# Values' steps before the keys', PSUM banks shared three and three, products one slot later

## The chip, the cores and the metric

The kernel runs on one NeuronCore of a Trainium2 chip. The metric is the device time of one execution in microseconds (us). Engines are named as in the profile: PE is the matrix engine's matmuls and PEld its weight loads, DVE, ACT and POOL are the vector, scalar and GpSimd engines, SP issues most DMAs.

## The reference

Three stages follow one another, all in fp32.

1. Attention: q, k, v are (8 batches, 8 heads, 576 positions, 64). Keys and values are averaged over groups of 8 positions, so that 72 pooled rows stand in each batch and head. `attn = softmax(q @ k_p.T / 8)`, output `attn @ v_p`. With the heads side by side it gives x, 4608 tokens by 512.
2. A dense layer: `h = x @ w_in` (512 to 2048), `g = max(0.01 * h, h)`, `y = g @ w_out` (2048 to 512).
3. A mixture of eight experts: `argmax(y @ w_gate)` picks one expert per token, which computes `max(y @ w1[e], 0) @ w2[e]` (512 to 1024 to 512), scaled by the softmax weight of the expert that was picked.

## The kernel before

**Precision.** Each fp32 operand of a large matmul is kept as a high part and a low part in a reduced format that PE takes at full rate, and a product is three matmuls (high by high, high by low, low by high). So nearly each result that leaves PSUM is written twice: ACT copies the high part (`act_copy`, L132), DVE subtracts it from the source for the low part (`sub`, L135).

**Slots.** Tokens are cut into 18 blocks of 256 (two tiles of 128). For each block b and each of 16 slices f of the hidden width there is one slot (b, f). The order is written out by hand in `seq`: blocks 0 and 1 are interleaved at the start, while the weights are converted; from b = 2 on the slots run in order. One turn of the main loop (from L1221) issues:

- `g1(b, f)`: 12 matmuls of 256 columns into one PSUM bank h; ACT writes 0.01 h to an SBUF tile g, DVE takes the maximum (L509; for b of 2 and more the result stays in the bank);
- the hooks of this slot (`run_slot`), set by `plan()` with `at(slot, function, ...)`;
- `g2` of an earlier slot (6 matmuls of 512 columns, L529, accumulated over f into the two banks y0 and y1 of the block): the list `pend` holds slots whose product into y is still to come, two of them in general, one at the edge of a block (f = 15 and f = 0);
- at f = 0 `y_evac` of the block before: two ACT copies and a DMA of y;
- `g_hi(b, f)` (ACT) and `g_lo(b, f)` (DVE), which write the two parts of g into one of two `ghl` tiles. `g_lo` is the last reader of the bank h.

All engines take their instructions in program order, so a late DVE instruction holds up everything behind it, and PE waits in turn for the data or the bank that it needs.

**Hooks.** The attention of the tiles of block b runs in the slots of block b-1: with i = 0 or 1 for the tile, `att_a` (4 transposes of q) at f = 0 and 7, `att_b` (scores, L380) at f = 2 and 9, `att_e` (exp) at 3 and 10, `att_n` (normalise, DVE) at 4 and 11, `att_c` (6 transposes, L412 and L418, then two DVE subtractions) at 6 and 13, and `att_av` (the values' product, L439, into x) for both at f = 15. Keys and values of a batch nb are loaded and pooled ahead of its first tile: parts 0 to 3 are keys, parts 4 and 5 the values' first 512 positions, part 6 the values' last 64 (the "rest"). Each part has three steps: `kv_load` (SP: 1, 2 or 8 DMAs), `kv_pool` (three DVE additions, and for part 6 a POOL multiplication, L300, into a further tile), `kv_use` (keys: one PE transpose, L313, and two ACT copies; values: ACT and DVE write `vm`, L325, or in `v_rest` `vr`). Raw parts share two `kv` tiles, so the load of a part waits for the use of the part two before it, and it is issued from that use. `att_b` needs the four keys, `att_av` needs all of `vm` and `vr`. In `plan()`, L1037 to L1056, the four key steps end just ahead of the first tile's `att_b`; the values' three stand 2, 4 and 6 slots after the last key step. For batches 2, 3, 6 and 7, whose first tile is the second of a block, this puts the rest's use into f = 14, one slot ahead of `att_av`. Other hooks: the experts' weights are split all along (`ps_split`: ACT copy, POOL subtraction of 128x512), DVE takes 16 dot products per block for the gate (L549), and small routing steps follow.

**PSUM.** There are eight banks. `pt("att")` hands out a0 and a1 in turn to everything that the hooks do on PE; `pt("h")` hands out h0 and h1, and from slot (2, 6) on y2 and y3 too, which blocks 0 and 1 no longer need. y0 and y1 hold the block's sums. In the profile a bank shows as a, h or y, so a `g1` can write "y".

**Third stage.** From about 1045 us on the experts run on gathered tokens with the same banks and `ghl` tiles: `p_g1`, `p_h`, `p_g2` on pairs of tiles, then single tiles (`m_g1`, `m_hT`, `m_g2`).

Of the kernel before, what the change touches and what calls it, by code (L numbers as in the profile page):

```python
# [21 lines left out]
def kernel(  # L22
# [13 lines left out]
    P = 128  # L36
# [60 lines left out]
    tri = pool.tile([P, P], BF16, name="tri")  # L97
    ones = pool.tile([P, P], BF16, name="ones")
    mask8 = pool.tile([64, E], F32, name="mask8")
    band = pool.tile([P, 112], F32, name="band")  # L100
    rep8 = pool.tile([64, E, E], F32, name="rep8")
    ebase = pool.tile([P, E], F32, name="ebase")
    iota8 = pool.tile([P, E], F32, name="iota8")
    rev8 = pool.tile([P, E], F32, name="rev8")
# [10 lines left out]
    def sb(shape, dt, tag, bufs=1):  # L115
        return (second[0] if tag in ("ps", "kv", "y4") else second[1] if tag in THIRD else pool).tile(shape, dt, name=tag, tag=tag, bufs=bufs)
# [73 lines left out]
    def kv_load(nb, i):  # L190
        if i < 4:
            t = sb([SP, 2, 512], F32, "kv", 2)
            nc.sync.dma_start(
                out=t, in_=k[nb, 2 * i:2 * i + 2].rearrange("h (m r) d -> m h (r d)", r=POOL)
            )
        elif i < 6:
            t = sb([P, 2, 512], F32, "kv", 2)
            for par in range(2):
                h0 = 4 * (i - 4) + par
                nc.sync.dma_start(  # L200
                    out=t[64 * par:64 * par + 64],
                    in_=v[nb, h0:h0 + 3:2, 0:512, :].rearrange("h (m r) d -> m h (r d)", r=POOL),
                )
        else:
            t = sb([64, 1, 512], F32, "kv", 2)
            for h in range(H):
                nc.sync.dma_start(
                    out=t[8 * h:8 * h + 8, 0, :],
                    in_=v[nb, h, 512:576, :].rearrange("(m r) d -> m (r d)", r=POOL),
                )  # L210
        kv_raw[nb, i] = t

    def kv_load0_k(nb):
        kt = sb([SP, H, 512], F32, "w03")
# [75 lines left out]
    def kv_pool(nb, i, eng=None):  # L290
        t = kv_raw[nb, i]
        eng = eng or nc.vector
        for w in (256, 128, 64):
            o = t[:, :, 0:w]
            if w == 64 and i < 4:
                o = t[:, 0, 256:384].rearrange("p (a d) -> p a d", a=2)
            eng.tensor_tensor(out=o, in0=t[:, :, 0:w], in1=t[:, :, w:2 * w], op=ALU.add)  # L297
        if i == 6:
            f = kv_raw[nb, 7] if nb < 2 else sb([64, H, 64], F32, "kv", 2)
            nc.gpsimd.tensor_tensor(  # L300
                out=f,
                in0=t[:, 0:1, 0:64].to_broadcast([64, H, 64]),
                in1=mask8.unsqueeze(2).to_broadcast([64, H, 64]),
                op=ALU.mult,
            )
            kv_raw[nb, 7] = f

    def kv_use(nb, i):
        t = kv_raw.pop((nb, i))
# [180 lines left out]
        act_copy(dh, w)  # L490
        sub(nc.vector, dl, w, f32(dh))

    g_raw, g_hl, y_ps = {}, {}, {}

    def g1(b, f):
        p = pt("h")
        xv = xs(b)
        n = 0
        for kk in range(KD):
            for l, r in ((0, 0), (0, 1), (1, 0)):  # L500
                nc.tensor.matmul(  # L501
                    p[:, 0:BLK], win(f)[:, kk, l], xv[:, kk, r], start=(n == 0), stop=(n == 3 * KD - 1)
                )
                n += 1
        t = sb([P, BLK], F32, "g", 2)
        h = p[:, 0:BLK]
        g = t if b < 2 else h
        act_copy(t, h, 0.01)
        nc.vector.tensor_tensor(out=g, in0=t, in1=h, op=ALU.max)  # L509
        g_raw[b, f] = g  # L510

    def g_hi(b, f):
        hl = sb([P, 2, BLK], F32R, "ghl", 2)
        act_copy(hl[:, 0], g_raw[b, f])
        g_hl[b, f] = hl

# [417 lines left out]
        return b  # L934

    def p_h(p, f, b):
        hl = sb([P, 2, BLK], F32R, "ghl", 2)
        nc.scalar.activation(hl[:, 0], b, AF.Relu)  # L938
        nc.vector.scalar_tensor_tensor(  # L939
            out=hl[:, 1], in0=b, scalar=0.0, in1=f32(hl[:, 0]), op0=ALU.max, op1=ALU.subtract  # L940
        )
        g_hl[p, f] = hl
# [83 lines left out]
    def plan():  # L1026
# [12 lines left out]
        for nb in range(2, B):  # L1039
            t = S * nb // P  # L1040
            b, i = divmod(t, TPB)
            sb_ = (b - 1) * NF + 2 + 7 * i
            use = []
            c = sb_ - 1
            while len(use) < 4:
                if c % NF in (1, 3, 5, 8, 10, 12, 14) and (not use or use[0] - c >= 3):
                    use.insert(0, c)
                c -= 1
            use += [use[3] + 2, use[3] + 4, use[3] + 6]
            for i in range(7):  # L1050
                at(use[i], kv_use, nb, i)
                if i + 2 < 7:
                    at(use[i], kv_load, nb, i + 2)
                at(use[i] - 2 + (i > 3), kv_pool, nb, i)
            at(max(use[0] - 6, 0), kv_load, nb, 0)
            at(use[0] - 5, kv_load, nb, 1)  # L1056
        for i in range(E * NCH):
            s = 34 + i * 9 // 5
            at(s, ps_load, i)
# [62 lines left out]
    with tc.manual_schedule():  # L1122
# [3 lines left out]
        cvp = first.enter_context(tc.tile_pool(name="cvp", bufs=1))  # L1126
        x1 = start.tile([P, KD * 2 * BLK], F32R, name="x1")
        e_t = [start.tile([P, 1024], U32, name=f"e{i}") for i in range(2)]
        ab_t = start.tile([P, 1024], BF16, name="ab_t")
        raw = [cvp.tile([P, 2, 1024], I32, name=f"raw{i}") for i in range(3)]  # L1130
        ebias = sb([P, 1], F32, "ebias")
        nc.vector.memset(ebias, -114688.0 * 65536.0)
# [88 lines left out]
        for s, (b, f) in enumerate(seq):  # L1221
            g1(b, f)
            if late:
                g_lo(*late.pop())
            run_slot(s)
            pend.append((b, f))
            end = s >= 2 * NF - 1 and (s % NF == NF - 1 or s % NF == 0)
            while len(pend) > (1 if end else 2):
                g2(*pend.pop(0))
            if s < 2 * NF:  # L1230
                conv(s, b, f)
            if b > 2 and f == 0:
                y_evac(b - 1)
            if (b, f) == (2, 6):
                banks["h"] += ["y2", "y3"]
            g_hi(b, f)
            if s < 2 * NF + LAG - 1:
                late.append((b, f))
            else:
                g_lo(b, f)  # L1240
            if (b, f) == (1, NF - 1):
                stack.close()
                second.append(ctx.enter_context(tc.tile_pool(name="third", bufs=1, side="right")))
                wgp = ctx.enter_context(tc.tile_pool(name="wgp", bufs=1, side="right"))
                wg_t.append(wgp.tile([P, E, DM], F32, name="wg"))
                nc.sync.dma_start(
                    out=wg_t[0].rearrange("p e d -> p (e d)"),
                    in_=wgT_d.rearrange("e d -> (e d)").partition_broadcast(P),
                )
            k0 = (NB - 1) * NF  # L1250
            if s == k0 + 7:
                early_1()
                w_regs(NR)
            if s == k0 + 12:
                early_2()
            if s >= k0 and f in (9, 10, 11, 15):
                w_load(0, [(9, 10, 11, 15).index(f)], regs[NR][0], None)
# [136 lines left out]
```

## Time and profile before

| | us |
|---|---|
| median of 3 runs | 1524.62 |
| lowest and highest | 1524.16, 1536.25 |
| the profiled execution, whole | 1533.83 |
| its span in the trace | 1532.1 |
| PE, DVE, ACT, POOL busy in it | 1468.8, 929.5, 619.1, 337.5 |

The profiled execution took 1.7 us more than its span. The first 180 us fill the pipeline and convert weights, blocks 2 to 17 of the dense layer take until about 1045 us, the experts the rest. An engine's busy time is the union of its instructions; a wait row says which engine and line sat idle, and whose result ended that. A row of instructions in order of time has start, duration, engine, line, operation, tiles, count, and in brackets the idle time before it.

### The profile page before, as it was taken

The page shows a single profiled execution, that of the slowest core. Times are in us where ns is not written, and L with a number is a line of the kernel's source. Part 1 is how long each engine was busy: PE and PEld are TensorE (multiplying, and loading weights), DVE is VectorE, ACT ScalarE, POOL GpSimd, SP SyncE. Part 2 cuts the span into 40 slices and gives each one's busy share as a digit, 9 for nine tenths or more (in the row PEclk, how much of TensorE's full clock was granted, in tenths as well). Part 3 has the DMA queues.
Part 4 walks back from the last instruction along what each step waited for, and adds up shares of the span by engine and source line. Part 5 has one row for each costly group of instructions (what it writes and reads, how often), then busy time and mean ns, then how long its engine had stood idle before and what let it go on. Part 6 is the DMA issues. An engine that isn't in the chain of part 4 may idle for free. (4 is left out here: it accounts for less than half of the span.)

```text
span 1532.1 us, 25665 instructions
## 1 busy us (share of the span) xinstructions
PE 1468.8 (96%) x9272; PEld 1315.8 (86%) x9272; DVE 929.5 (61%) x2387; ACT 619.1 (40%) x1412; POOL 337.5 (22%) x318
## 2 busy tenths in 40 slices
PE   4698999999999999999999999999999999999998
PEld 3587889999898898899989899988899999988886
DVE  6999588878869888877867867674212112111111
ACT  4666344544444444544444444332222222222222
POOL 4002022222332222222222332111211211201111
PEclk8799999999999999999989999999999999999999
DMA  9543346446445555545636544143611118566160
GB/s 216 148 152 92 111 132 195 163 161 194 162 152 182 169 178 170 174 148 176 193 120 199 172 146 164 49 174 104 275 49 49 56 35 338 202 234 263 42 258 19
DMA packets 121385, 238.05 MB, mean 155 GB/s; under 512 B 56845, under 2 KB 65041, under 8 KB 117544
## 3 DMA queue, kind: packets, MB, share of 16 engines
q1 hardware_dynamic: 90312, 139.81, 29.2%
q10 hardware_dynamic: 23328, 76.56, 13.3%
q0 software_dynamic: 7616, 20.01, 3.9%
q8 instruction: 75, 1.23, 0.3%
q14 instruction: 54, 0.44, 0.1%
HBM read 317.78 MB, written 87.38 MB: 264 GB/s over the span
## 5 line engine op out<-in xcount | busy, mean ns | idle before, releaser
L529 PE MATMUL y<-w,ghl 128*128 128x512 f32 x1728 | 464.4, 406 | 0.9 <-DVE spf L781 0.6
L529 PEld LDWEIGHTS y<-w,ghl 128*128 128x128 f32 x1728 | 309.7, 191 | 58.5 <-DVE ghl L135 3.1
L135 POOL TENSOR_TENSOR ps<-ps 128x512 f32<-128x512 f32 x128 | 181.8, 1421 | 473.6 <-ACT ps L132 391.2
L501 PEld LDWEIGHTS h<-x_t,w 128*128 128x128 f32 x1776 | 236.0, 192 | 32.3 <-DVE w L135 13.6
L501 PE MATMUL h<-x_t,w 128*128 128x256 f32 x1776 | 242.7, 286 | 16.4 <-DVE w L135 12.2
L549 DVE CUSTOM_DVE_ANT_0 junk<-y,wg 128x512 bf16<-128x512 f32 x256 | 201.3, 786 | 2.0
L501 PEld LDWEIGHTS y<-x_t,w 128*128 128x128 f32 x1488 | 193.2, 189 | 9.6
L501 PE MATMUL y<-x_t,w 128*128 128x256 f32 x1488 | 196.2, 282 | 0.0
L951 PE MATMUL y<-w,ghl 128*128 128x512 f32 x672 | 175.1, 399 | 1.0 <-DVE ghl L939 1.0
L951 PEld LDWEIGHTS y<-w,ghl 128*128 128x128 f32 x672 | 119.6, 189 | 22.3 <-DVE ghl L939 1.4
L132 ACT ACTIVATE g<-h 128x256 f32<-128x256 f32 x164 | 62.8, 383 | 151.7 <-PE h L501 140.9
L1007 POOL DMA_INDIRECT out_dram<-kv,sidx x40 | 40.3, 1007 | 372.3 <-ACT kv L1006 188.1
L939 DVE SCALAR_TENSOR_TENSOR ghl<-h,ghl 128x256 fp32r<-128x256 f32 x56 | 23.8, 425 | 136.0 <-ACT ghl L938 136.0
L509 DVE TENSOR_TENSOR h<-g,h 128x256 f32<-128x256 f32 x132 | 56.0, 424 | 77.1 <-ACT g L132 76.4
L135 DVE TENSOR_TENSOR at_t<-a,at_t 128x512 fp32r<-128x512 f32 x62 | 42.7, 688 | 86.9 <-ACT at_t L132 86.4
L132 ACT ACTIVATE ghl<-h 128x256 fp32r<-128x256 f32 x132 | 50.7, 384 | 94.3 <-PE y L529 47.0
L132 ACT ACTIVATE ps<-ps 128x512 fp32r<-128x512 f32 x128 | 80.4, 628 | 15.5 <-DMA ps<-in_moe_w_dram 9.8
L132 ACT ACTIVATE ghl<-y 128x256 fp32r<-128x256 f32 x124 | 47.3, 382 | 94.1 <-DVE y L509 50.6
L132 ACT ACTIVATE g<-y 128x256 f32<-128x256 f32 x124 | 47.4, 382 | 61.4 <-PE y L501 53.8
L135 DVE TENSOR_TENSOR ghl<-h,ghl 128x256 fp32r<-128x256 f32 x132 | 55.5, 420 | 24.8 <-ACT ghl L132 24.5
L616 POOL DMA_INDIRECT lst<-ent,six x36 | 37.7, 1048 | 148.3 <-DVE six L615 110.0
L297 DVE TENSOR_TENSOR kv<-kv 72x512 f32<-72x512 f32 (+8 forms) x126 | 67.9, 539 | 3.2
(272 smaller groups left out, 2140.7 us busy)
## 6 DMA issues: line engine op xcount, KB each, us to landing
w<-wsp SPq DMA_DIRECT2D x108, 2048.0 KB
wsp<-ps ACTq DMA_DIRECT2D x128, 512.0 KB
ps<-in_moe_w_dram SPq DMA_DIRECT2D x128, 256.0 KB
y_d<-y ACTq DMA_DIRECT2D x18, 512.0 KB
raw<-in_moe_w_in_dram SPq DMA_DIRECT2D x16, 512.0 KB
raw<-in_moe_w_out_dram SPq DMA_DIRECT2D x16, 512.0 KB
q<-in_q_dram SPq DMA_DIRECT2D x28, 256.0 KB
kv<-in_k_dram SPq DMA_DIRECT2D x24, 288.0 KB
```

The lines of the kernel that those rows point to most:

```text
L132: nc.scalar.activation(o, i, AF.Copy, scale=scale)
L135: eng.tensor_tensor(out=o, in0=a, in1=b, op=ALU.subtract)
L297: eng.tensor_tensor(out=o, in0=t[:, :, 0:w], in1=t[:, :, w:2 * w], op=ALU.add)
L501: nc.tensor.matmul(p[:, 0:BLK], win(f)[:, kk, l], xv[:, kk, r], start=(n == 0), stop=(n == 3 * KD - 1))
L509: nc.vector.tensor_tensor(out=g, in0=t, in1=h, op=ALU.max)
L529: nc.tensor.matmul(y_ps[b, i], hl[:, l, i * P:i * P + P], wout(f)[:, r], start=(f == 0 and l + r == 0), stop=(last and l == 1),)
L549: nc.vector.tensor_tensor_reduce(out=jk, in0=y_sb[b][:, i], in1=wg_t[0][:, e], scale=1.0, scalar=0.0, op0=ALU.mult, op1=ALU.add, accum_out ...
L616: nc.gpsimd.indirect_dma_start(out=lst, out_offset=bass.IndirectOffsetOnAxis(ap=ix[:, 0:1], axis=0), in_=ent[:, i, :], in_offset=None, bou ...
L939: nc.vector.scalar_tensor_tensor(out=hl[:, 1], in0=b, scalar=0.0, in1=f32(hl[:, 0]), op0=ALU.max, op1=ALU.subtract)
L951: nc.tensor.matmul(o_ps[2 * p + i], hl[:, l, i * P:i * P + P], w[:, r], start=(f == 0 and l + r == 0), stop=(f == 7 and l == 1),)
L1007: nc.gpsimd.indirect_dma_start(out=out, out_offset=bass.IndirectOffsetOnAxis(ap=sidx[:, t:t + 1], axis=0), in_=o, in_offset=None, bounds_c ...
```

## The change

- In `plan()`, for batches 3 to 7 the values' three steps stand 7, 5 and 3 slots ahead of the first key step. They were 2, 4 and 6 slots behind the last. Batch 2 keeps its places. The seven steps of a batch are sorted by slot; the first two loads are issued 6 and 5 slots ahead of the first step, each further load at the use two steps before it.
- The rest's pooled product is written into the second half of its own raw tile and takes no third `kv` tile.
- From slot (2, 6) on y2 goes to the h banks and y3 to the attention banks: three and three, where there were four and two.
- From block 3 on `pend` holds three slots. At f = 15 it is cut to two, at f = 0 to one, so a block's last slots have their products as 12, 13 at f = 15 and 14, 15 at f = 0, and its first product comes after `g1` of f = 3.
- `ghl` gets a third tile at slot (3, 0), in the pool "third", and the tiles are handed out in turn. To make room, `band` and `rep8` move to the conversion pool, one of the two g tiles to the start pool (one is left after slot (1, 15), whose `g_lo` is no longer put off by a slot).

```diff
         else:
-            t = sb([64, 1, 512], F32, "kv", 2)
+            t = sb([64, 2, 512], F32, "kv", 2)
...
+            kv_raw[nb, 7] = t[:, 1].rearrange("p (h d) -> p h d", h=H)
+        kv_raw[nb, i] = t if i < 6 else t[:, 0:1]
...
-            f = kv_raw[nb, 7] if nb < 2 else sb([64, H, 64], F32, "kv", 2)
+            f = kv_raw[nb, 7]
...
+    g_t = [pool.tile([P, BLK], F32, name="g0")]
+    hl_t = [pool.tile([P, 2, BLK], F32R, name=f"ghl{i}") for i in range(2)]
+    hl_n = [0]
+
+    def hl_next():
+        hl_n[0] += 1
+        return hl_t[hl_n[0] % len(hl_t)]
...
-        t = sb([P, BLK], F32, "g", 2)
+        t = g_t[len(g_n) % len(g_t)]
+        g_n.append(0)
...
-        hl = sb([P, 2, BLK], F32R, "ghl", 2)
+        hl = hl_next()
...
-            use += [use[3] + 2, use[3] + 4, use[3] + 6]
-            for i in range(7):
-                at(use[i], kv_use, nb, i)
-                if i + 2 < 7:
-                    at(use[i], kv_load, nb, i + 2)
-                at(use[i] - 2 + (i > 3), kv_pool, nb, i)
-            at(max(use[0] - 6, 0), kv_load, nb, 0)
-            at(use[0] - 5, kv_load, nb, 1)
+            rows = [use[3] + 2, use[3] + 4, use[3] + 6] if nb == 2 else [use[0] - 7, use[0] - 5, use[0] - 3]
+            steps = sorted([(c, i) for i, c in enumerate(use)] + [(c, 4 + i) for i, c in enumerate(rows)])
+            for n, (c, i) in enumerate(steps):
+                at(c, kv_use, nb, i)
+                if n + 2 < 7:
+                    at(c, kv_load, nb, steps[n + 2][1])
+                at(c - 2 + (i > 3), kv_pool, nb, i)
+            for n in range(2):
+                at(steps[0][0] - 6 + n, kv_load, nb, steps[n][1])
...
-            end = s >= 2 * NF - 1 and (s % NF == NF - 1 or s % NF == 0)
-            while len(pend) > (1 if end else 2):
+            deep = 2 if b < 3 else 3
+            if s >= 2 * NF - 1:
+                deep -= (f == NF - 1) + (deep - 1) * (f == 0)
+            while len(pend) > deep:
                 g2(*pend.pop(0))
...
+            if (b, f) == (3, 0):
+                hl_t.append(second[1].tile([P, 2, BLK], F32R, name="ghl2"))
             if (b, f) == (2, 6):
-                banks["h"] += ["y2", "y3"]
+                banks["h"] += ["y2"]
+                banks["att"] += ["y3"]
             g_hi(b, f)
-            if s < 2 * NF + LAG - 1:
+            if s < 2 * NF + LAG - 1 and (b, f) != (1, NF - 1):
                 late.append((b, f))
...
             if (b, f) == (1, NF - 1):
+                g_t.pop(0)
                 stack.close()
```

## Rows read from the trace of the kernel before

**Rows 1.** The page: busy time of the engines.

```profile
PE 1468.8 (96%) x9272; PEld 1315.8 (86%) x9272; DVE 929.5 (61%) x2387; ACT 619.1 (40%) x1412; POOL 337.5 (22%) x318
```

**Rows 2.** Windows of blocks 6, 8, 10, 11, 12: length, busy per engine, clock, DMA.

```profile
400.30:451.74 51.44, 51.44 (x344) 47.13 (x342) 38.24 (x106) 23.75 (x56) 16.19 (x12) 1.00 0.49 165
...
504.55:559.51 54.96, 52.19 (x344) 47.12 (x343) 46.48 (x126) 26.32 (x65) 15.18 (x12) 1.00 0.51 166
...
612.40:668.51 56.11, 53.92 (x368) 48.86 (x367) 45.91 (x125) 26.80 (x66) 15.49 (x12) 1.00 0.48 158
668.51:720.06 51.55, 51.55 (x345) 47.23 (x343) 40.57 (x109) 24.38 (x58) 14.16 (x11) 1.00 0.54 176
720.06:780.18 60.12, 58.46 (x362) 53.34 (x361) 46.92 (x131) 27.32 (x70) 15.55 (x12) 0.91 0.51 152
```

**Rows 3.** Waits of PE and PEld from 200 to 1010 us: total, times, longest.

```profile
PE a L361 <- DVE at_t L135: 5.6, 4, 2.2
PE a L439 <- DVE vr L135: 4.5, 4, 1.7
PE a L418 <- DVE rtmp L606: 1.0, 1, 1.0
PE a L313 <- DVE at_t L135: 0.4, 1, 0.4
...
PEld a L361 <- DVE at_t L135: 6.4, 4, 2.4
PEld a L439 <- ACT vr L132: 4.9, 4, 1.8
```

**Rows 4.** Windows with a granted clock (third from last) below 1.00.

```profile
770.00:780.00 10.00, 10.00 (x37) 8.94 (x37) 4.09 (x10) 2.74 (x6) 1.38 (x1) 0.50 0.13 53
882.00:889.00 7.00, 7.00 (x28) 6.23 (x28) 3.36 (x9) 2.21 (x4) 1.67 (x1) 0.53 0.12 50
```

**Rows 5.** Order of time: the rest of batch 6, and batch 2's wait.

```profile
766.81 1.28 POOL L300 TENSOR_TENSOR kv<-kv,mask 64x512 f32<-64x512 f32 x1 [7.98 <-DMA ps<-in_moe_w_dram]
...
768.58 1.02 DVE L135 TENSOR_TENSOR vr<-kv,vr 32x256 fp32r<-32x256 f32 x1 [0.70 <-ACT vr L132]
...
769.75 0.40 PE L439 MATMUL a<-rm_t,vr 128*128 128x128 f32 x1 [1.66 <-DVE vr L135]
...
288.02 0.30 PE L439 MATMUL a<-rm_t,vr 128*128 128x128 f32 x1 [0.69 <-DVE vr L135]
```

**Rows 6.** Order of time in slots (10, 6) and (10, 7).

```profile
633.18 2.12 DVE L325 SCALAR_TENSOR_TENSOR vm<-kv,vm 64x128 fp32r<-64x128 f32 x2
633.51 1.31 POOL L135 TENSOR_TENSOR ps<-ps 128x512 f32<-128x512 f32 x1
636.61 0.69 DVE L135 TENSOR_TENSOR at_t<-a,at_t 128x512 fp32r<-128x512 f32 x1
637.35 0.66 PE L361 MATMUL a<-ident,q 128*128 128x128 f32 x4 [2.19 <-DVE at_t L135]
```

**Rows 7.** Window of batch 6's values, instructions on tile kv alone.

```profile
746.00:771.00 25.00, 0.00 (x0) 0.00 (x0) 6.88 (x15) 2.90 (x8) 1.28 (x1) 0.98 0.58 173
```

**Rows 8.** Line 325 by itself: duration in ns, least, median, most.

```profile
L325 DVE SCALAR_TENSOR_TENSOR vm<-kv,vm x24: 273/288/1795, 273.1 to 874.2; 64x128 fp32r<-64x128 f32 x24
```

**Rows 9.** Order of time at the edge of blocks 10 and 11.

```profile
671.79 3.02 PE L501 MATMUL y<-x_t,w 128*128 128x256 f32 x24
671.84 1.07 ACT L132 ACTIVATE y<-y 128x512 f32<-128x512 f32 x2
673.88 0.42 DVE L135 TENSOR_TENSOR ghl<-h,ghl 128x256 fp32r<-128x256 f32 x1
675.53 1.64 PE L529 MATMUL y<-w,ghl 128*128 128x512 f32 x6
```

**Rows 10.** Order of time at the first single tile of the experts.

```profile
1383.74 0.68 DVE L135 TENSOR_TENSOR x_t<-a,x_t 128x512 fp32r<-128x512 f32 x1
...
1384.29 2.09 PE L969 MATMUL y<-w,x_t 128*128 128x512 f32 x8
```

More of the change, by code (lines that the diff above doesn't have):

```diff
@@ L99 @@
     mask8 = pool.tile([64, E], F32, name="mask8")
-    band = pool.tile([P, 112], F32, name="band")
-    rep8 = pool.tile([64, E, E], F32, name="rep8")
     ebase = pool.tile([P, E], F32, name="ebase")
@@ L210, in kv_load @@
                 )
-        kv_raw[nb, i] = t
+            kv_raw[nb, 7] = t[:, 1].rearrange("p (h d) -> p h d", h=H)
+        kv_raw[nb, i] = t if i < 6 else t[:, 0:1]
     def kv_load0_k(nb):
@@ L305, in kv_pool @@
             )
-            kv_raw[nb, 7] = f
     def kv_use(nb, i):
@@ L491, in w_conv2 @@
         sub(nc.vector, dl, w, f32(dh))
-    g_raw, g_hl, y_ps = {}, {}, {}
+    g_raw, g_hl, y_ps, g_n = {}, {}, {}, []
+    g_t = [pool.tile([P, BLK], F32, name="g0")]
[4 more added lines that the diff above has]
+        return hl_t[hl_n[0] % len(hl_t)]
     def g1(b, f):
@@ L936, in p_h @@
     def p_h(p, f, b):
-        hl = sb([P, 2, BLK], F32R, "ghl", 2)
+        hl = hl_next()
         nc.scalar.activation(hl[:, 0], b, AF.Relu)
@@ L1128 @@
         e_t = [start.tile([P, 1024], U32, name=f"e{i}") for i in range(2)]
+        g_t.insert(0, start.tile([P, BLK], F32, name="g1"))
         ab_t = start.tile([P, 1024], BF16, name="ab_t")
+        band = cvp.tile([P, 112], F32, name="band")
+        rep8 = cvp.tile([64, E, E], F32, name="rep8")
         raw = [cvp.tile([P, 2, 1024], I32, name=f"raw{i}") for i in range(3)]
```

## The prediction

> **What bounds the kernel now.** I read the page first: PE is busy for 96% of the span [rows 1], so some 63 us are left in which it is not, and those alone can be won. Most lie in the first 180 us, which the change hardly touches. Then the windows, one per block of the dense layer [rows 2]: blocks 6 and 11 take 51.44 and 51.55 us and PE is busy in all of it. That is the floor: DVE has 38 to 41 us of work there, ACT 24, both hidden. Block 8 takes 54.96 us with 2.77 idle, block 10 has 2.19 idle, block 12 1.66. Third, the waits of PE from 200 to 1010 us [rows 3]. Four kinds make 11.5 us: att_a's transposes wait for the subtraction that frees their attention bank (5.6 us, four times, at f = 7 of blocks 7 to 10), two more wait for such a bank (1.0 and 0.4), and the values' product waits for the rest `vr` (4.5, four times, at f = 15 of blocks 3, 5, 12 and 14). Last, the order of time shows why. In block 12 POOL's multiplication, ACT's copies and DVE's subtraction of the rest run one after another while PE stands at its first `vr` [rows 5]. In block 10 DVE is late because the values' steps share slots with tile work; the transposes at 637.35 need only a bank, and wait 2.19 us for the subtraction at 636.61 [rows 6].
>
> **The execution and the median.** The sum has to be made against the profiled execution, 1533.8 us, but this one has two stretches at 1.2 GHz, half the clock, right behind waits for `vr`: 10 us at 0.50 and 7 us at 0.53 [rows 4]. What they cost is the lost half: 10 x 0.50 + 7 x 0.47 = 8.3 us. 1533.8 - 8.3 = 1525.5, the median within 0.9 us. So I take the median's runs to be free of them, and credit the change with nothing for them.
>
> **Values' steps ahead (batches 3 to 7).** The work is the same: per batch 12 DMAs on SP, one POOL multiplication, and on DVE 6.88 us in 15 instructions, on ACT 2.90 in 8 [rows 7]. Only its place changes.
> - Batches 3, 6 and 7: the rest is now ready a whole block before `att_av`, so its waits go: 4.5 less the 0.69 of batch 2, which keeps its place [rows 3, 5], -3.8 us.
> - What takes its place: the work goes into f = 6 to 11 of blocks 4, 11 and 13. Block 11 then has 40.57 + 6.88 = 47.5 us of DVE work in 51.55, 92%, and block 12 falls to 40. Still under the floor, so the cover holds; a DVE that is late by more than the g chain allows would show as waits of g1 for a bank.
> - Batches 4 and 5: the steps leave f = 2 to 7 of blocks 8 and 10, where the two long bank waits are, and go to f = 13 to 15 and 0 to 2 at the edges of blocks 6 and 7, and of 8 and 9. Behind the edge two slots of PE are short (no product), so DVE falls behind there. Bounds: nothing, or all that blocks 8 and 10 now lose (2.77 + 2.19 = 5.0 [rows 2]). I take 1.0, near the lower end, since the bank that made the late subtraction a wait is no longer the one needed next, and `pend` is deeper.
> - SP: each batch still has five loads that wait for a use, the same count in the same queue; a first value has five slots from load to pooling, later parts at least three, as before. Behind such a waiting load stand the experts' weight loads and q, due several slots later. POOL no longer waits for a third tile. 0.
>
> **Third attention bank.** att_a at f = 7, the small transposes of att_c and the keys' transpose now find a bank that was given back a hook earlier: 5.6 + 1.0 + 0.4 = -7.0 us by PE's idle time. PEld stands longer at the same places (6.4 against 5.6, 4.9 against 4.5 [rows 3]), since the array has to be filled again. So the two terms lie between 10.8 and some 12.2 us; I take 11.5.
>
> **Three h banks, products one slot later, third ghl.** With 51.44 / 16 = 3.2 us per slot: `g_hi(f)` waits for the product that frees its ghl tile, at the end of its own slot, before and after. Before, `g2(f)` needs the low part one and a half slots later (4.8 us), the bank is needed after three. Now `g2(f)` has two and a half slots, but the bank is needed by `g1(f + 3)` two slots later (6.4 us). The tightest term gets 1.6 us looser: 0, or some tenths of gain. At the edge the row of today is [rows 9]: the two y copies start at 671.84, the low part of f = 0 is done at 674.30, 2.5 us after the last product; the first product starts at 675.53, 1.2 us to spare. After the change the same chain starts as the last product ends, and g1 of f = 1 and 2 and att_b (671.79 to 675.53, 3.7 us) are its cover again, this time for g1 of f = 3, which needs the bank. Cost 0, with 1.2 us in reserve.
>
> **The rest.** The moved g tile, `band`, `rep8` and the earlier `g_lo(1, 15)` change one place in DVE's order: 0. In the experts a bank wait of m_hT (1.0 us in the trace) falls away, but the g1 behind it needs `x_t`, whose subtraction runs from 1383.74 to 1384.42, while that g1 starts at 1384.29 anyway [rows 10]: 0, at most 1.0.
>
> **Sum.** 1524.6 - 11.5 + 1.0 = 1514.1, so **1514 us**, 0.7% less. The upper bounds of all gains (12.2, the tail's 1.0, no new lag, half a us of run-to-run spread) give 1511; three us more for waits under 0.1 us that no row lists, 1508.
>
> **A rule against it.** Line 325 takes 288 ns in the median and up to 1795 [rows 8]; the long one began at 633.18, and POOL's subtraction of 1.31 us ran from 633.51 to 634.82, inside its time [rows 6]. So a DVE instruction that reads two SBUF tiles can stand while POOL reads. The Trainium skill, SBUF — State Buffer, "Who interferes with whom", says it as a rule: such a DVE instruction and a GpSimd instruction that reads SBUF exclude each other, and whichever comes second waits for the whole of the first. The trace agrees, by the 1.5 us above. By that rule the values' additions, all of two SBUF inputs, would each be a chance to lose the POOL instruction's time in their new slots.
>
> **Rivals.**
> 1. *DVE falls behind at the edge with batches 4 and 5* (0.18). Price: each of the three pooling steps and the use meets POOL once, 1.5 us each, 6 us of lag; of that some 2 is covered by the reserve, so 4 us in blocks 7 and 9, 8 in all: 1514 + 8 = 1522. For it: POOL is busy for 16 of 51 us, DVE has little room at f = 1 to 3. Against: the meetings are as likely in the old slots, and the chain has looser slack away from the edge.
> 2. *The edge itself binds* (0.06), the other sign. The low part of f = 0 would be later than 3.7 us behind the last product at every edge, in blocks 4 to 17. It decides from 1.2 us of delay on; at 3.0 us (two POOL meetings in the routing's DVE chain) PE loses 1.8 x 14 = 25 us: 1524.6 - 11.5 + 25 = 1538, and waits that long may bring back the half clock. Against: y's copies are first in ACT's order and today's block floors show no wait there.
> 3. *The waits move and nothing is won* (0.06). If DVE, not the bank, sets att_a's time, PE waits a slot later for g, and the 7.0 come back while 3.8 stay: 1521. Against: blocks 6 and 11 run at the floor with 40 us of DVE work.
> 4. *More is won* (0.10): 1508 and below, where the lists of waits leave much out.
>
> The forecast as summed has 0.60. What a measurement of this kernel can tell from no change is about 1%, 15 us. 1509 divides faster from same: 0.11 (rival 4 and a tail of the forecast); slower, over 1540, needs rival 2 beyond its price: 0.04; within 1%: 0.85. Range for 8 in 10: 1508 to 1522, which takes in the forecast with its bounds and most of rival 1.
>
> **What would show it.** Right: in 200 to 1010 us no wait of L361 or L418 for `at_t` or `rtmp`, L439 for `vr` once (block 3), blocks 8, 10 and 12 at 52.2 to 53.9, no stretch below 2.4 GHz there. Rival 1: blocks 7 and 9 longer than 53, waits of g1 (L501 before, its new line after) for DVE's ghl at f = 3 to 6. Rival 2: that wait at f = 3 of every block. The forecast is wrong if blocks 4, 6, 11 and 13 leave their floor by a us or more, or if the rows of the experts change.

## The result: 0.8% faster, 12 us, most of it from a term that the prediction held at nothing

The changed kernel takes 1517.85 us (median of 17 runs, 1515.23 to 1523.09), the kernel before 1530.01 in as many runs beside it (1524.16 to 1540.05). The ratio is 0.9918 [0.9906, 0.9931]. Of the three runs shown first two, 1524.16 and 1524.62, are the lowest of the 17, so their median was 5.4 us too low. The profiled execution took 1521.41 us, its span is 1519.7, so it stands 12.4 us below before's 1533.83.

PE's busy time fell by 15 us against [rows 1], with the same instructions, and its idle time rose by 2. The page's line:

```profile
PE 1454.0 (96%) x9272; PEld 1298.1 (85%) x9272; DVE 931.6 (61%) x2387; ACT 609.7 (40%) x1412; POOL 337.3 (22%) x318
```

The windows of blocks 4, 6, 7, 8, 9, 10, 11, 12 and 15 after the change (stretch, length, then PE, PEld, DVE, ACT and POOL busy with their counts, granted clock, DMA share, GB/s):

```profile
298.72:350.50 51.78, 51.38 (x344) 46.53 (x343) 45.84 (x122) 26.34 (x66) 16.22 (x12) 1.00 0.63 198
403.64:454.41 50.77, 50.77 (x344) 46.41 (x342) 40.66 (x110) 23.88 (x58) 14.92 (x12) 1.00 0.63 179
454.41:508.47 54.06, 52.00 (x347) 46.69 (x345) 48.71 (x126) 26.90 (x68) 15.65 (x13) 1.00 0.59 178
508.47:560.00 51.53, 51.12 (x344) 46.62 (x343) 42.39 (x114) 23.69 (x59) 13.85 (x11) 1.00 0.61 170
560.00:615.05 55.05, 52.08 (x346) 46.71 (x345) 50.31 (x129) 26.69 (x68) 15.57 (x12) 1.00 0.54 177
615.05:668.03 52.98, 52.98 (x369) 48.34 (x368) 39.24 (x110) 24.57 (x58) 14.22 (x11) 1.00 0.47 155
668.03:720.85 52.82, 51.70 (x344) 46.51 (x343) 46.07 (x122) 26.27 (x66) 15.19 (x12) 1.00 0.58 185
720.85:773.79 52.94, 52.94 (x362) 48.58 (x361) 43.55 (x119) 25.00 (x62) 14.40 (x11) 1.00 0.48 159
...
878.71:929.47 50.76, 50.76 (x343) 46.41 (x342) 38.40 (x106) 23.15 (x56) 15.93 (x12) 1.00 0.48 161
```

Against [rows 2], blocks 8, 10 and 12 fell by 3.4, 3.1 and 7.2 us. The last two lie in the forecast 52.2 to 53.9, block 8 below it; 5 of block 12's 7.2 us are the half clock that it had before ([rows 4]). Blocks 7 and 9 rose to 54.06 and 55.05, and DVE has 48.7 and 50.3 us of work there. Before, they were:

```profile
451.74:504.55 52.81, 51.98 (x346) 47.50 (x345) 43.92 (x114) 25.04 (x62) 15.06 (x12) 1.00 0.56 182
559.51:612.40 52.89, 52.03 (x346) 47.51 (x345) 43.98 (x115) 24.97 (x62) 14.58 (x11) 1.00 0.56 177
```

The row that matters most is block 6. It waits for nothing before and after, PE is busy in all of it with the same 344 records, and it is 0.67 us shorter. Block 15 shows the same (51.44 before), though DVE's work there is unchanged and in block 6 it grew by 2.4 us, so it is no matter of what the hooks do.

PE's waits from 200 to 1010 us after the change (engine, bank, line waited by whose result; total, times, longest):

```profile
PE h L507 <- DVE ghl L133: 6.5, 6, 3.7
PE y L507 <- DVE ghl L133: 2.4, 2, 1.6
PE y L311 <- PE h L507: 1.0, 2, 0.5
PE a L437 <- DVE vr L133: 0.9, 1, 0.9
PE a L410 <- DVE pn L399: 0.7, 2, 0.4
```

They sum to 11.5 us, and the four kinds of [rows 3] summed to 11.5 (two small ones more made 12.0). The attention banks' waits are gone, the rest `vr` is waited for once; in their place g1 (L507) waits for the low part of g (L133) that frees its bank. The waits were exchanged, not won.

The half clock of [rows 4] is gone from 770 and 882 us, and stands elsewhere. Windows of the stretches at 0.50 after the change:

```profile
209.80:213.20 3.40, 3.05 (x14) 3.06 (x15) 0.29 (x1) 0.03 (x1) 0.00 (x0) 0.50 0.02 5
291.70:298.50 6.80, 6.80 (x23) 5.74 (x23) 2.49 (x6) 1.65 (x4) 1.68 (x1) 0.50 0.00 0
1029.00:1032.40 3.40, 3.01 (x9) 2.57 (x10) 1.38 (x2) 0.83 (x2) 0.00 (x0) 0.50 1.04 439
```

For the account the span is cut at the end of the last g1 of block 17, 1036.35 us before and 1023.17 after (the same columns as above; before, then after):

```profile
180.00:1036.35 856.35, 843.51 (x5578) 768.94 (x5577) 676.44 (x1870) 393.54 (x967) 229.51 (x172) 0.99 0.50 163
1036.35:1532.10 495.75, 487.21 (x2900) 428.69 (x2898) 101.17 (x252) 119.63 (x247) 81.64 (x80) 1.00 0.39 147
...
180.00:1023.17 843.17, 830.28 (x5571) 753.93 (x5570) 681.21 (x1870) 387.34 (x967) 229.02 (x172) 0.99 0.52 166
1023.17:1519.70 496.53, 485.80 (x2906) 426.24 (x2904) 98.40 (x252) 116.45 (x247) 81.83 (x80) 0.99 0.39 148
```

The dense stage is 13.2 us shorter. PE's idle time in it is the same, 12.8 and 12.9 us, so the waits gave nothing. Half clock cost 8.3 us before and half of 10.2 now: some 3.2. One product of six matmuls, 1.4 us, now stands behind the cut, since `pend` is deeper. The rest, some 8.6 us, is the floor of the blocks. The experts look 0.8 us longer, but they carry that product (1.4), 2.2 us more idle time and 1.7 us of half clock; without these they are some 4.5 us shorter. So of the 12.4 us in the trace the shorter floor, in both stages, made about 13, fewer stretches at half clock 1.5 more, and the idle time at the experts' start took 2 of it back.

**The three new waits.** The longest stands in slot (2, 7). PE's g1 and products in order of time, after the change:

```profile
204.83 1.64 PE L536 MATMUL y<-w,ghl 128*128 128x512 f32 x6
210.15 2.93 PE L507 MATMUL h<-x_t,w 128*128 128x256 f32 x12 [3.67 <-DVE ghl L133]
```

Banks are handed out by a counter modulo the length of the list. At (2, 6) the list grows from two to three while the counter runs on: 39 modulo 2 is 1, and 40 modulo 3 is 1. The bank h1 is handed out twice in a row, so g1 of (2, 7) has to wait until slot (2, 6) has been evacuated, its low part too. The clock falls to half at 209.8, 3.3 us after PE's last matmul had ended, and the matmuls run at that clock until 213.2.

The second is in block 9, at f = 4, DVE and PE in order of time:

```profile
569.12 0.68 DVE L556 CUSTOM_DVE_ANT_0 junk<-y,wg 128x512 bf16<-128x512 f32 x1
...
569.84 2.65 DVE L556 CUSTOM_DVE_ANT_0 junk<-y,wg 128x512 bf16<-128x512 f32 x1
...
572.42 0.41 DVE L133 TENSOR_TENSOR ghl<-y,ghl 128x256 fp32r<-128x256 f32 x1
...
572.89 0.38 PE L507 MATMUL y<-x_t,w 128*128 128x256 f32 x1 [1.59 <-DVE ghl L133]
```

and POOL in the same stretch:

```profile
569.33 1.37 POOL L299 TENSOR_TENSOR kv<-kv,mask 64x512 f32<-64x512 f32 x1 [3.92 <-DVE kv L296]
...
570.66 1.27 POOL L133 TENSOR_TENSOR ps<-ps 128x512 f32<-128x512 f32 x1
```

The gate's dot product, two SBUF inputs, takes 0.68 us and then 2.65. The second began 0.5 us after POOL's multiplication of the values (L299) had begun, and lasted until both POOL instructions were over. The low part behind it on DVE is late by those 2 us, and PE waits 1.59. It is the mechanism of the first rival, in the place it named; only the DVE instruction that stood is the gate's and not one of the poolings.

The third is the start of the experts (PE, after):

```profile
1027.95 0.66 PE L923 MATMUL a<-ident,ps 128*128 128x128 f32 x4 [1.99 <-DMA ps<-y_d,gidx]
...
1029.39 1.09 PE L923 MATMUL y<-ident,ps 128*128 128x128 f32 x4 [0.79 <-DMA ps<-y_d,gidx]
```

With `pend` one deeper, the last block's product of slice 14 comes after `p_xT` of the first pair in PE's order. It was cover for the gathers; now PE stands 2.8 us for them, 3.4 in all of the experts where it was 0.6, and half clock follows. The 1.0 us wait of `m_hT` behind [rows 10] is gone, as the prediction held possible, and m_g1 waits 0.6 us for `x_t` where it had not waited.

### The profile page after: what moved, and what is told of

It is laid out like the page before. It is cut to its first block, busy times and chain, and to the rows that moved or that the text cites. A ratio compares the mean times of both kernels' runs of the same rounds, so it can differ in the third digit from the quotient of the medians.

```text
span 1519.7 us, 25944 instructions
## 1 busy us (share of the span) xinstructions
PE 1454.0 (96%) x9272; PEld 1298.1 (85%) x9272; DVE 931.6 (61%) x2387; ACT 609.7 (40%) x1412; POOL 337.3 (22%) x318
## 5 line engine op out<-in xcount | busy, mean ns | idle before, releaser
L536 PE MATMUL y<-w,ghl 128*128 128x512 f32 x1728 | 459.3, 404 | 0.8 <-DVE ghl L133 0.8
L536 PEld LDWEIGHTS y<-w,ghl 128*128 128x128 f32 x1728 | 309.8, 191 | 58.4 <-DVE ghl L133 1.8
L507 PEld LDWEIGHTS h<-x_t,w 128*128 128x128 f32 x2268 | 293.6, 191 | 43.0 <-DVE w L133 13.7
L507 PE MATMUL h<-x_t,w 128*128 128x256 f32 x2268 | 304.0, 284 | 22.7 <-DVE w L133 12.4
L133 POOL TENSOR_TENSOR ps<-ps 128x512 f32<-128x512 f32 x128 | 181.2, 1415 | 482.8 <-ACT ps L130 436.6
L507 PEld LDWEIGHTS y<-x_t,w 128*128 128x128 f32 x996 | 126.6, 188 | 9.7 <-DVE ghl L133 3.2
L507 PE MATMUL y<-x_t,w 128*128 128x256 f32 x996 | 130.0, 280 | 2.4 <-DVE ghl L133 2.4
L130 ACT ACTIVATE g<-h 128x256 f32<-128x256 f32 x205 | 78.2, 382 | 130.6 <-PE h L507 120.1
L130 ACT ACTIVATE ghl<-h 128x256 fp32r<-128x256 f32 x173 | 66.2, 383 | 128.8 <-DVE h L516 80.8
L516 DVE TENSOR_TENSOR h<-g,h 128x256 f32<-128x256 f32 x173 | 72.9, 421 | 58.8 <-ACT g L130 58.7
L133 DVE TENSOR_TENSOR ghl<-h,ghl 128x256 fp32r<-128x256 f32 x173 | 72.5, 419 | 26.9 <-ACT ghl L130 24.7
L133 DVE TENSOR_TENSOR at_t<-a,at_t 128x512 fp32r<-128x512 f32 x48 | 33.0, 688 | 87.0 <-ACT at_t L130 83.9
L1013 ACT ACTIVATE kv<-y,gate 128x512 f32<-128x512 f32 x40 | 26.0, 686 | 94.4 <-PE y L958 67.0
L937 PEld LDWEIGHTS h<-at_t,w 128*128 128x128 f32 x456 | 58.0, 188 | 3.0
```

The source lines that it names most:

```text
L130: nc.scalar.activation(o, i, AF.Copy, scale=scale)
L133: eng.tensor_tensor(out=o, in0=a, in1=b, op=ALU.subtract)
L507: nc.tensor.matmul(p[:, 0:BLK], win(f)[:, kk, l], xv[:, kk, r], start=(n == 0), stop=(n == 3 * KD - 1))
L536: nc.tensor.matmul(y_ps[b, i], hl[:, l, i * P:i * P + P], wout(f)[:, r], start=(f == 0 and l + r == 0), stop=(last and l == 1),)
L937: nc.tensor.matmul(b, w[:, l], xp(p)[:, kk, r], start=(n == 0), stop=(n == 3 * KD - 1))
```

## The experiments

Ratios are against the kernel before, run beside each on the same chip; its medians were 1529.56, 1532.43 and 1532.45 us in the three groups (the first four runs, the next four, the last four), so times of different groups compare to some 3 us only. "The repaired kernel" is the one from which the second group starts.

**Is it the place of the weights?** The change moves tiles (`band`, `rep8`, g, ghl), and with them the weights' tiles in SBUF. Worked out from the order of allocation, those of slices 0 to 7 begin at 0 modulo 128 bytes of a partition before and at 64 after, those of slices 8 to 15 at 32 and at 96; `x_t`, `at_t` and `vm` begin at 0 in both. The two ghl tiles move too, from 0 to 96. The first experiment gives the weights of before their new place and changes nothing else in the program (ghl then begins at 64, as far from the weights as before):

```diff
     acc = pool.tile([P, TPB, E], BF16, name="acc")
+    pad0 = pool.tile([P, 16], F32, name="pad0")
```

> The schedule of before, with 64 bytes of unused SBUF ahead of the weights' tiles, so that these start 64 or 96 bytes past a multiple of 128 as they do after the change (before: 0 or 32), while x_t stays at a multiple of 128. Place theory (the plain blocks fell from 51.45 to 50.77 us because g1's matmuls follow each other in 113 to 117 ns instead of 120, and that comes from where the weights lie beside x_t): plain blocks of 50.7 us, g1's spacing as after the change, same waits as before, 11 to 15 us less than before, about 1514. Schedule theory (the faster spacing comes from three h banks or from products one slot later): plain blocks stay at 51.45, time within 2 us of before.

1521.75 us, 0.993 [0.9907, 0.9953]. 64 unused bytes make the kernel before 0.7% faster: 8 us by the medians, 11 by the ratio, where 11 to 15 were expected. Its block 6, window:

```profile
399.75:450.60 50.85, 50.85 (x343) 46.57 (x342) 38.35 (x106) 23.70 (x56) 15.98 (x12) 1.00 0.50 167
```

It was 51.44. The floor falls without the new schedule. The experts, cut as above, take 491.9 us in place of 495.8.

**The same pad in the changed kernel** takes the weights back to 0 and 32:

> The changed kernel with 64 bytes of unused SBUF ahead of the weights' tiles, which puts them back on 0 or 32 past a multiple of 128. Place theory: plain blocks return to 51.4 us, g1's spacing to 120 ns, the time rises by 11 to 15 us over the changed kernel, to about that of before (1526 to 1531), so the new order of the work by itself is worth nothing. Schedule theory: plain blocks stay at 50.8, time as after the change, 1515 to 1519.

1527.94 us, 0.998 [0.996, 1.0], 10 us more than the change. The window of its block 6:

```profile
405.06:456.35 51.29, 51.29 (x343) 46.90 (x342) 41.29 (x110) 23.99 (x58) 15.55 (x12) 1.00 0.56 177
```

So the schedule by itself, with the old place, is worth little: 3 us, and the interval reaches from 0 to 6.

**Is it the weights' own address, or their distance to the other operand?** In before, `x_t` and `at_t` move by 64 bytes and the weights stay where they were modulo 128:

```diff
+    pad0 = pool.tile([P, 16], F32, name="pad0")
     x_t = pool.tile([P, KD * 2 * BLK], F32R, name="x_t")
     at_t = pool.tile([P, NPAIR * 2 * BLK], F32R, name="at_t")
+    pad1 = pool.tile([P, 16], F32, name="pad1")
```

> The schedule of before with x_t and at_t moved up by 64 bytes and the weights left where they were modulo 128. If it is the distance between the two operands of a matmul that counts, g1's spacing falls as in the changed kernel (plain blocks 50.7 us, time 11 to 15 us less). If it is the weights' own address, nothing changes (51.45 us). Schedule theory: nothing changes.

1521.9 us, 0.994 [0.9918, 0.9962]. Its block 6, window:

```profile
400.47:451.36 50.89, 50.89 (x343) 46.62 (x342) 38.34 (x106) 23.73 (x56) 15.99 (x12) 1.00 0.51 167
```

The same fall from the other side, so what counts is how the two operands lie to each other, not the weights' address alone. The time fell by 8 to 9 us, again less than the 11 to 15 expected.

**The two mishaps repaired** (the collision at (2, 6), the order at the experts' start), in the changed kernel:

```diff
                 banks["att"] += ["y3"]
+                turn["h"] += 1
...
+        while len(pend) > 1:
+            g2(*pend.pop(0))
         p_xT(0, 0)
```

> The changed kernel with two repairs: the turn of the h banks is moved on by one where the third comes in at slot (2, 6), so that g1 of (2, 7) doesn't get the bank that g1 of (2, 6) has just filled; and block 17's product of f = 14 stands ahead of the experts' first transposes again. Expected: PE's wait of 3.7 us at the start of slot (2, 7) and the half clock behind it (3.4 us at 0.50) go, 5.4 us; of the 2.8 us at the first gathered tiles about 1.4 go. 1517.9 - 6 = about 1511. If the wait at (2, 7) were DVE's lateness and not the bank, it would stay.

1509.1 us (1508.64 to 1511.95), 0.9853 [0.9809, 0.9896]: the best kernel of the study, 9 us faster than the change, where 6 or 7 were expected. Block 2 falls from 60.18 to 54.70 us, which is the collision with its half clock. Block 3 falls from 56.22 to 52.57: the stretch at 291.7 is gone, at which neither repair was aimed, and no stretch of this execution's dense stage is at half clock. PE's waits from 200 to 1010 us there:

```profile
PE h L507 <- DVE ghl L133: 4.5, 5, 1.5
PE y L507 <- DVE ghl L133: 2.4, 3, 0.8
```

The waits of blocks 7 and 9 are still there (54.05 and 54.99 us). The next four start from this kernel and undo one part each.

**Values back behind the keys:**

```diff
-            rows = [use[3] + 2, use[3] + 4, use[3] + 6] if nb == 2 else [use[0] - 7, use[0] - 5, use[0] - 3]
+            rows = [use[3] + 2, use[3] + 4, use[3] + 6]
```

> The repaired changed kernel (1509.1 us) with the values' steps of every batch behind the keys' again; banks three and three, products three slots behind. By the prediction's sum: PE's waits for vr return in blocks 5, 12 and 14 (3.8 to 4.5 us), with half clock behind two or three of them (3.4 us each), the lag in blocks 7 and 9 goes (about 2.7 and 3.7 us there): net +2 to +6, 1511 to 1515. Rival (DVE's lateness moves with its work, and hosts 4, 11 and 13 lose their waits as well, 1.7, 1.8 and 3.1 us): waits cancel, and only the half clock is left: -3 to +3, 1506 to 1512.

1519.67 us (7 runs, 1511.07 to 1524.94), 0.992 [0.9889, 0.9951], 10 us more than the repaired kernel and above both ranges. The profiled execution, at 1513.0, is among its shortest. Its waits for `vr` (PE):

```profile
PE y L437 <- DVE vr L133: 3.3, 2, 2.1
PE a L437 <- DVE vr L133: 2.2, 2, 1.3
```

and its windows at half clock:

```profile
760.90:764.30 3.40, 3.40 (x12) 2.72 (x11) 1.42 (x4) 1.61 (x3) 1.18 (x1) 0.51 0.01 2
...
866.80:873.60 6.80, 6.80 (x25) 5.93 (x24) 2.85 (x7) 1.98 (x4) 1.68 (x1) 0.50 0.05 20
```

The waits for `vr` come back, and half clock behind them; blocks 7 and 9 fall back to 51.7 us, 8 and 10 rise to 54.1 and 54.6. In this execution the 5.1 us of lost clock are more than the difference to the repaired kernel (1.1 us over its 1511.95). That the longer executions hold more such stretches is borne out in part by the mean granted clock of each, which is on record without a trace: 0.985 at 1511.07 us, 0.978 at 1521.27, 0.977 at 1524.94, against 0.984 to 0.986 in the repaired kernel; but 1519.58 has the 0.981 of the 1513.01 that was profiled. So lost clock seems to be most of the 10 us (the median's 0.981 against 0.986 is 7.6 us of the span), not all.

**Banks back to four and two:**

```diff
-                banks["h"] += ["y2"]
-                banks["att"] += ["y3"]
-                turn["h"] += 1
+                banks["h"] += ["y2", "y3"]
```

> The repaired changed kernel with four h banks and two attention banks as before; values ahead, products three slots behind. By the prediction: L359 waits for at_t at f = 7 and L410 or L416 for a bank again, some 7 us, 1516. Rival (with the values' steps gone from f = 2 to 7, DVE is not late there and the bank is free in time): less than 3 us of such waits, and with four h banks the waits of g1 for ghl (7.8 us in the repaired kernel) shrink: 1503 to 1509, so three and three costs rather than gains.

1528.21 us, 0.9979 [0.9959, 1.0]: 19 us more than the repaired kernel, far above both expectations. Its waits of PE:

```profile
PE a L311 <- DVE at_t L133: 10.1, 4, 3.0
PE a L311 <- issue: 3.8, 2, 1.9
```

Here the keys' transposes (L311) wait, up to 3 us each, in blocks 4, 7, 9, 11 and 13, which take 55 to 57 us; four stretches, 17.0 us, are at half clock and cost 8.5 of the 19 us. With the values ahead of the keys the third attention bank carries much more than the 7.0 us of waits that it removes from before.

**Two slots of `pend`, two ghl tiles** (`deep = 2`; the third tile is allocated and not used):

> The repaired changed kernel with two products outstanding and two ghl tiles as before; values ahead, three and three banks. By the prediction 0 to some tenths per block, +0 to +3 us: 1509 to 1512. Rival (the two product-free slots behind each block's edge let PE run into DVE's lateness): waits of g1 for ghl at f = 3 to 5 of blocks 7 and 9 fall from 2.7 and 3.7 us to under 1, 1504 to 1507.

1512.87 us, 0.9894 [0.9855, 0.9933]. The interval overlaps the repaired kernel's. Its longest wait:

```profile
PE y L536 <- DVE ghl L133: 6.3, 7, 1.4
```

The products (L536) now wait 6.3 us for the low part and 0.9 for the high one; in the repaired kernel g1 waited 6.9 for the low part. Blocks 2 to 16 sum to 792.1 us against 791.1. The deeper `pend` only changes which matmul stands; a value of some us can't be excluded.

**Place once more**: 96 bytes ahead of the weights of slices 8 to 15, so that they too lie at 64:

```diff
         ebias = sb([P, 1], F32, "ebias")
+        sb([P, 3, H], F32, "st")
```

> The repaired changed kernel with the small tile st allocated ahead of the weights of f = 8 to 15 instead of behind them: those weights' tiles move up by 96 bytes and lie 320 bytes past x_t modulo 512, as those of f = 0 to 7 do; nothing else moves. If place sets g1's spacing, its sum over the slot above the ideal falls at f = 8 to 15 from 113 to about 82 ns, 0.25 us per block: plain blocks 50.77 to 50.53 us, 4 us in the dense layer and 1 to 2 in the experts, 1503 to 1505. If f = 8 to 15 are slower for another reason, no change (1508 to 1510).

1510.95 us, 0.9867 [0.9832, 0.9901]; the time is the repaired kernel's, though this profiled execution has 6.8 us at half clock (at 285.9) and the other has none. The floor fell a little (block 6):

```profile
398.13:448.82 50.69, 50.69 (x344) 46.35 (x342) 41.15 (x110) 24.00 (x58) 15.53 (x12) 1.00 0.58 180
```

50.69 against 50.77, and 50.53 was expected. Of the slices that moved, 9, 14 and 15 fell from 117 to the 114 ns between two matmuls that most of slices 1 to 7 have; 8, 10 and 13 fell to 116 only, and 11 and 12 rose a little, to 118. Slices 4 and 7, whose weights did not move, rose from 114 to 116. The distance of the two operands modulo 128, or 512, is therefore not the whole rule.

The last four apply parts alone to before, or move the values again.

**Values ahead alone, in before** (the kv tile and `rows`/`steps` of the change):

> The kernel before with the values' steps ahead of the keys' (batches 3 to 7) and nothing else: two attention banks, four h banks, two products outstanding, weights where they were. By the prediction: the waits for vr go in blocks 5, 12 and 14 (3.8 us), the half clock behind them too (in the runs that make before's median about 5 us more), 7 to 10 us less than before, ratio 0.994 to 0.996. Rival from the run with two attention banks: the keys' transposes (L313) and att_a now wait for the attention bank in blocks 4, 7, 9, 11 and 13, 8 to 14 us with their own half clock, so that the time is within 5 us of before or above it, ratio 0.998 to 1.003.

1534.94 us, 1.0008 [0.9992, 1.0024]: nothing, as the rival had it. Its waits of PE:

```profile
PE y L529 <- DVE ghl L135: 5.5, 7, 1.3
PE a L313 <- DVE at_t L135: 4.7, 4, 1.4
PE a L361 <- DVE at_t L135: 3.1, 2, 1.5
PE a L439 <- DVE vr L135: 0.7, 1, 0.7
```

The wait for `vr` falls from 4.5 to 0.7, exactly the 3.8 us forecast, and the waits of products and transposes take its place. DVE's work is the same and its crowded stretch has moved: blocks 4, 7, 9, 11 and 13 are 2.4 to 4.4 us longer than before, 16 in all (block 7 takes 56.35), and blocks 5, 8, 10, 12 and 14 are 18 shorter. The half clock of [rows 4] is gone as well, so that its 8.3 us were lost again with the rest.

**Three banks each alone, in before** (with the counter repaired):

```diff
-                banks["h"] += ["y2", "y3"]
+                banks["h"] += ["y2"]
+                banks["att"] += ["y3"]
+                turn["h"] += 1
```

> The kernel before with three attention and three h banks from slot (2, 6) on (turn repaired) and nothing else. By the prediction: the bank waits of L361, L418 and L313 go, 7.0 us, the waits for vr and their half clock stay: ratio 0.995. Rival (DVE is late there anyway and PE then waits for g in g2 or for the h bank): 2 to 4 us, ratio 0.997 to 0.999.

1523.55 us, 0.9948 [0.9925, 0.9972], -8 us. Its waits:

```profile
PE y L439 <- DVE vr L135: 2.3, 2, 1.2
PE a L439 <- DVE vr L135: 1.8, 2, 1.1
PE y L529 <- DVE ghl L135: 1.6, 2, 1.3
```

All of the attention banks' waits are gone, and only 1.6 us come in their place: PE's idle time from 180 us to the last g1 falls from 12.8 to 6.7. The 8 us are not the bank's alone. This profiled execution lost 1.7 us to half clock where before's lost 8.3, though the waits for `vr` are still there.

**Another place for the values** (the repaired kernel, steps 8, 6, 3 or 15, 13, 10 slots ahead, chosen to leave the edges of blocks 7 and 9):

```diff
-            rows = [use[3] + 2, use[3] + 4, use[3] + 6] if nb == 2 else [use[0] - 7, use[0] - 5, use[0] - 3]
+            if nb == 2:
+                rows = [use[3] + 1, use[3] + 4, use[3] + 5]
+            else:
+                rows = [use[0] - d for d in ((8, 6, 3) if i else (15, 13, 10))]
```

> The repaired changed kernel (1509.1 us) with the values' steps at other slots: uses at f = 6, 8 and 11 of the block two ahead for all batches (poolings at f = 5, 7 and 10, where no tile step loads DVE), and the rest of batch 2 one slot earlier. If the waits for ghl in blocks 7 and 9 (2.7 and 3.7 us over their floor of 51.3) come from the values' steps at the edge of the block, these blocks fall to 51.3 to 51.8, blocks 6 and 8 rise by up to 1 us each, blocks 4, 11 and 13 keep or lose up to 1 us, and block 3's wait for vr (0.9) goes: 3 to 6 us less, 1503 to 1506. Rival (the key steps alone make DVE late there): no change, 1508 to 1511.

1519.32 us, 0.9904 [0.9877, 0.9931]: missed, 8 us by the ratio and 10 by the medians behind the repaired kernel. Windows of its blocks 6 and 8 (blocks 7 and 9 take 51.70 and 51.71):

```profile
396.20:451.47 55.27, 52.86 (x343) 47.61 (x342) 44.47 (x121) 25.34 (x64) 16.23 (x13) 0.97 0.59 180
...
503.17:561.26 58.09, 53.60 (x344) 47.75 (x343) 48.00 (x126) 25.53 (x65) 14.10 (x12) 0.97 0.60 172
```

Blocks 7 and 9 are down to 51.7 as meant, and blocks 6 and 8 have risen by 4.5 and 6.6 us, of which 1.7 each are half clock (0.97 in both rows). The wait moved with the work.

**The same, with the 96 bytes ahead of the weights of slices 8 to 15:**

> The kernel with the other slots, and with the tile st ahead of the weights of f = 8 to 15 (96 bytes further up). The first look at this place alone showed plain blocks at 50.69 us where 50.53 was expected, and half clock that hid the rest. If place is worth what the plain blocks show, 0.1 us per block: 1 to 2 us less than the same kernel without it; if what g1's spacing showed at f = 8, 9, 14 and 15 (113 to 85 ns) holds everywhere, 4 us less.

1517.3 us, 0.9892 [0.9866, 0.9918]: 2 us less than without, which these intervals don't tell apart.

## Why the prediction was right in its time and wrong in its account

The time lay in the range, 3.9 us above the forecast of 1514; the ratio of 0.8% stands beside a forecast of 0.7%. That was luck. The sum started from 1524.6, 5.4 us below before's later median, and with the old place of the weights its 10.5 us of gain come to 3. The terms under it:

- **"The moved g tile, `band`, `rep8` and the earlier `g_lo(1, 15)` change one place in DVE's order: 0"** is the step that failed most. It looked at the instructions of the moved tiles and not at what the move does to the addresses of PE's operands. The pad is worth 8 to 11 us in before and 10 in the changed kernel, more than the rest together. The prediction also called 51.44 us the floor of a block; with the same instructions it is 50.77.
- **Values ahead, -3.8.** The removed term was sized right to the tenth: alone, the waits for `vr` fell from 4.5 to 0.7. What was wrong is the sentence "the cover holds". In all three places that were tried DVE's 6.9 us per batch made PE wait in the blocks where they met the tile work, and alone the part is worth 0 (ratio 1.0008). The third rival's condition, that DVE's lateness and not the bank decides, held for this part.
- **Third attention bank, -7.0.** Confirmed: alone, PE's idle time falls by 6.1 us and the time by 8, in which the half clock has a part. In the repaired kernel going back costs 19, 8.5 of them half clock, since the values ahead make the keys' transposes need it too. The two terms were added as if independent; they are not.
- **Lag at the edge with batches 4 and 5, +1.0 of 0 to 5.0**, mis-sized: blocks 7 and 9 lose 2.1 and 3.0 us of PE's time, 5.0 together, the upper bound, with g1 waiting for `ghl` at f = 4 and 5, as the first rival said. The POOL meeting that it priced at 1.5 us cost 2 in block 9. The Trainium skill, SBUF — State Buffer, "Who interferes with whom", says that the second of such a pair waits for the whole of the first; the trace agrees and goes further: the 2.65 us of an instruction of 0.68 cover the rest of one POOL instruction and the whole of the next. Besides, blocks 4, 11 and 13 left the floor of 50.8 by 1.0, 2.0 and 1.0 us, which the prediction named as a sign against it, as it did a change in the rows of the experts.
- **Three h banks, deeper `pend`, third ghl: 0.** Nothing at the edge, as argued: the floor of block 6 shows no wait. But the step didn't follow the counter over the change of the list: 3.67 us of wait plus 1.7 of lost clock at (2, 7). And "0, at most 1.0" for the experts looked at the single tiles of the end and not at the first pair, where the deeper `pend` takes the cover from the gathers: 2.8 us and 1.7 of clock. Both repaired give 9 us, 3.4 of them from a stretch of half clock at which the repairs were not aimed.
- **Half clock, 0 credited.** The median of three runs agreed with the profiled execution less its 8.3 us by chance; over 17 runs the median is 1530, between the two. Half clock does weigh on before's runs: of the 25 beside the first group of experiments the shortest, 1523.53 us, has a mean granted clock of 0.987 and the longest, 1541.09, of 0.974. How much of the median it is stays open. In the changed kernel the time does not go with the clock (1515.23 us at 0.981, 1523.09 at 0.983). The change itself has 10.2 us at half clock in its dense stage, against "no stretch below 2.4 GHz there".

So the sum came out because 8 to 11 us that were not foreseen stood against gains that were lost again. The second rival (the edge itself binds) did not occur.

## What to carry to other kernels

Where a change moves an allocation, work out where PE's two operands lie before and after, and try a pad of 64 bytes on the old kernel: it may be worth more than the edit. Here the waits whose cause was a late engine moved with that engine's work, and the waits for a bank went away with another bank. When a list that is handed out in turn changes its length, write down the next two indices.

## What the runs showed of the hardware

**Spacing of matmuls.** Twelve matmuls of 256 columns, in order of time, before:

```profile
926.08 1.59 PE L501 MATMUL h<-x_t,w 128*128 128x256 f32 x12
927.50 0.39 PE L529 MATMUL y<-w,ghl 128*128 128x512 f32 x1
```

and after:

```profile
566.01 1.53 PE L507 MATMUL h<-x_t,w 128*128 128x256 f32 x12
567.38 0.65 PE L378 MATMUL y<-kT,qT 128*128 128x144 f32 x4
```

From the first start to the next instruction's it is 1.42 us before (slice 12 of block 15) and 1.37 after (slice 2 of block 9): 118 and 114 ns for each matmul. Over the plain blocks, 6 and 15 among them, the mean from one matmul of a slice to the next is 118 to 121 ns before, in every slice. After it is 113 to 114 in slices 1, 2 and 4 to 7 and 116 to 118 in slices 8 to 15; the values' product, whose operands did not move, kept 120 in both. In before with the pad, and with `x_t` moved, slices 1 and 2 come down to 113 to 115, 4 to 7 to 118 only, 8 to 15 to 117 or 118; the changed kernel with the pad has 118 nearly everywhere. That the relative place has a part in it is shown by these kernels from both sides. It is not all, since the slices differ at the same distance; which distances are good is open.

**Half clock behind short waits.** Stretches at half clock stand behind waits for `vr` in before ([rows 4]) and in the kernel with the values behind the keys, and behind the 3.67 us at (2, 7). After the change one of 6.8 us, at 291.7, follows a wait of only 0.91 us for `vr`, which ended at 289.91. The 1.59 us of block 9 have none behind them, nor have the 2.19 us of [rows 6] in before, nor the waits of up to 1.5 us of the repaired kernel, among them the same wait of 0.9 us for `vr`. So a wait's length alone doesn't decide; what else does is open.
